# The buffer of each tile named by the plan's own times in a kernel with an S4D convolution and linear attention

## The chip, the core and the metric

The kernel runs on one core of a Trainium2 chip. TensorE (PE) multiplies matrices and writes into PSUM, a memory of eight banks; VectorE (DVE) and ScalarE (ACT) read PSUM and empty it; GpSimd (POOL) works on SBUF alone; SyncE (SP) issues the transfers (DMA). The engines run side by side, each through its own row of instructions, and wait for each other by semaphores. In the profile PEld is the loading of weights into TensorE, which overlaps the matmuls (PE).

The metric is the time of one execution on the device, in microseconds (us).

## What is computed

Two independent parts stand side by side in the output. A is a long convolution over 2048 positions with a kernel made from S4D parameters, by FFTs. B is linear attention with a learned feature map over 32 heads of 18 columns.

```python
def _A_ref(u, log_A_real, A_imag, C_real, C_imag, log_dt, D_skip):
    L = u.shape[1]
    dt = jnp.exp(log_dt)
    A = -jnp.exp(log_A_real) + 1j * A_imag
    C = (C_real + 1j * C_imag) * dt[:, None]
    P = jnp.exp((A * dt[:, None])[:, :, None] * pos[None, None, :])
    K = 2.0 * jnp.einsum("dn,dnl->dl", C, P).real
    y = irfft(rfft(u_t, 2 * L) * rfft(K, 2 * L)[None], 2 * L)[:, :, :L]
    return y.transpose(0, 2, 1) + u * D_skip[None, None, :]

def _B_ref(x, wqkv, w_phi, wo):
    q, k, v = ...
    pq = jnp.einsum("bhsd,hdf->bhsf", q, w_phi)
    pk = jnp.einsum("bhsd,hdf->bhsf", k, w_phi)
    phi_q = jnp.concatenate([_softmax(pq), _softmax(-pq)], axis=-1)
    phi_k = jnp.concatenate([_softmax(pk), _softmax(-pk)], axis=-1)
    kv = jnp.einsum("bhsf,bhsd->bhfd", phi_k, v)
    z = jnp.einsum("bhsf->bhf", phi_k)
    o = einsum(phi_q, kv) / (einsum(phi_q, z) + 1e-6)
    return o.reshape(B, S, D) @ wo

return jnp.concatenate([a, b], axis=-1)
```

Shapes: 2048 positions, 576 columns, 128 states; all float32.

## The kernel before

**Attention.** The 2048 rows are taken in 16 tiles of 128. A key tile multiplies x by the key and value weights, in three groups of 14 matmuls (`gemm`, line 537), each into one PSUM tile; DVE, ACT and POOL make the two softmaxes; 32 small matmuls (ps<-e,v, line 620) add to the sums over keys. Then 16 query tiles do the same for the queries, transpose, divide, and multiply by the output weights. Products are made more exact by splitting each factor into a rounded part and a rest (wh and wl for the weights).

**Convolution.** `u_first` (line 742) and `first` (line 730) are first FFT steps of the input and of the kernel; `group` (line 905) makes the kernel's values from waves (cs) and magnitudes, with three matmuls ps<-sel,mg (line 915) whose results ACT turns into exponentials (line 916) and DVE multiplies into cs and E (lines 922 to 927). `product` (line 981) takes eight blocks for each half of the columns: 16 matmuls ps<-ub,ff (line 1003), kernel-side matmuls ps<-kb,fk (line 1022), complex products into ac, and 16 matmuls back. `last` (line 1059) is the final step.

**The order.** All of this is recorded first, as a list of 2972 operations with an engine, an estimated length, the operations they depend on, and the tiles (`Buf`) they touch. The string `ORDER` says in which order they are laid out, and so the row of each engine; parts of A and B are interleaved in it. `Plan.run` walks through that order once. For each operation it works out an estimated start, the latest of its engine's time, its inputs' ends and the free times of the buffers that it takes, and then emits the instruction. Where it estimates that PE would stand idle, it emits filler matmuls into the tile about to be written (line 215).

**The buffers.** Every tile has a tag. A tag has a fixed number of buffers: `ps` has eight, the eight PSUM banks, through which all matmul results go; `small` seven, `cs` four, `e` and `x9` three, most others one or two. The plan keeps, for each tag, a list of the times at which its buffers come free (`free`). When a tile is first touched, the smallest of these times is taken off the list and delays the operation's estimated start; when the tile's last use has been emitted, the estimated end of its uses goes back on the list. These are numbers alone: the tile itself is asked of a pool with as many buffers as the tag has, and the pool chooses which one it gets. The framework then adds the waits: whoever first writes the tile waits for all readers of the tile that was in that buffer before.

Of the kernel before, what the change touches and what calls it, by code (L numbers as in the profile page):

```python
# [143 lines left out]
class Buf:  # L144


    def __init__(self, tag, shape, dt):
        self.tag, self.shape, self.dt = tag, shape, dt
        self.writers, self.readers, self.left, self.end, self.t = [], [], 0, 0.0, None
# [9 lines left out]
class Plan:  # L159
# [10 lines left out]
        self.ops, self.pools, self.free, self.unit, self.part = [], {}, {}, None, None  # L170

    def tag(self, name, pool, n):
        self.pools[name], self.free[name] = pool, [0.0] * n

    def at(self, name, k=0):
        self.unit, self.part = (name, k), None
# [4 lines left out]
    def buf(self, tag, shape, dt=F32):  # L181
        return Buf(tag, shape, dt)
# [35 lines left out]
    def run(self, order):  # L218


        ops = self.ops
        if sorted(int(x.rstrip("*")) for x in order) != list(range(len(ops))):
            raise RuntimeError("the order does not hold every operation once")
        at = {e: 0.0 for e in self.LAG}
        port = dict(dve=0.0, pool=0.0)
        self.warm, self.short, self.long = False, 0.0, 0.0

        def idle(t):
            self.short += max(0.0, t)
            if self.short > IDLE:  # L230
                self.warm, self.long = False, 0.0

        def busy(t, share):
            self.short = max(0.0, self.short + t * (1.0 - 2.0 * share))
            self.long += t * share
            if self.long > WARM and self.short <= IDLE:
                self.warm = True
        table, dma, end, mode = None, 0.0, [None] * len(ops), None
        for x in order:
            k, second = int(x.rstrip("*")), x.endswith("*")  # L240
            o = ops[k]
            e, cost = o[5] if second else o[:2]
            s = max([at[e], *(end[d] for d in o[3])])
            for b in o[4]:
                if b.t is None:
                    fr = self.free[b.tag]
                    b.t0 = min(fr)
                    fr.remove(b.t0)
                    s = max(s, b.t0)
                    b.t = self.pools[b.tag].tile(b.shape, b.dt, name=b.tag, tag=b.tag)  # L250
            if o[8] and e in port:
                s = max(s, port["pool" if e == "dve" else "dve"])
            if e == "act" and o[6] and table and o[6] != table:
                s += 1420.0
            table = o[6] or table
            fill = 0
            if e == "pe":
                t = at[e]
                if o[11] is not None:
                    t = max(t, 0.0 if o[12] else o[11].t0, self.zero_at)  # L260
                    idle(t - at[e])
                    c = FILL if self.warm else 2 * FILL
                    fill = max(0, min(100, int((s - 150.0 - t) // c)))
                    busy(fill * c, 1.0)
                    t += fill * c
                idle(s - t)
                cost = (cost + (20.0 if o[10] == mode else 95.0 + o[10][1] / 1.2)) * (1 if self.warm else 2)
                mode = o[10]
                busy(cost, o[7])
            self.emit(o, e, fill)  # L270
            at[e] = s + (560.0 if e == "sp" else cost)
            if o[8] and e in port:
                port[e] = at[e]
            if e == "sp":
                dma = max(dma, s + 1050.0) + cost
            end[k] = (max(dma, s + 1050.0 + 1.85 * cost) if e == "sp" else at[e]) + self.LAG[e]
            for b in o[4]:
                b.left -= 1
                b.end = max(b.end, end[k])
                if not b.left:  # L280
                    self.free[b.tag].append(b.end)
        self.end, self.time = end, max(end)


# [12 lines left out]
def c_dma(nbytes, run=4096):  # L297
    return nbytes / run * (0.35 + 0.0029 * run)
# [112 lines left out]
def body(tc, nc, i, out, ctx):  # L411
    pl = Plan()
    pe, dve, act, pool, sp = nc.tensor, nc.vector, nc.scalar, nc.gpsimd, nc.sync

    def tags(spec, space=None):
        kw = {} if space is None else dict(space=space)
        for n, names in spec.items():
            p = ctx.enter_context(tc.tile_pool(name=f"x{n}{len(pl.pools)}", bufs=n, **kw))
            for t in names.split():
                pl.tag(t, p, n)  # L420

    tags({1: "zero ident w1 w3 hp dsk kvb fT wh wl ks E sel dt th cre cim ax ay mx mn ld ldc",
          2: "v1 o ot pi mg ff ub kb zo us2 ac yo zi", 3: "e fk x9", 4: "cs", 7: "small"})
    tags({8: "ps"}, space=PSUM)
    tags({1: "gd kz", 5: "dram", 16: "xd"}, space=DRAM)
    B, op = pl.buf, pl.op

# [677 lines left out]
```

## Time and profile before

| | |
|---|---|
| three runs, median | 586.39 us |
| three runs, lowest and highest | 583.33 and 587.55 us |
| the profiled execution | 580.1 us |
| its span, from the first to the last instruction | 578.1 us |
| mean granted TensorE clock | 0.999 |

The lines that carry the prediction are shown in it. A line of the timeline gives start, length, engine, line of the kernel, operation, output<-inputs, shapes, a count of instructions merged, and in brackets how long the engine stood idle before it and what ended that. Nearly all matmuls have line 429, a helper, so they are told apart by their tiles: ps<-wh,x is a matmul of x with a weight. Copies out of PSUM have line 434.

### The profile page before, as it was taken

What the parts mean: (1) busy time and instruction counts of PE and PEld (TensorE: products, weight loads), DVE (VectorE), ACT (ScalarE), POOL (GpSimd) and SP (SyncE); (2) the same over time, 40 slices, a digit from 0 to 9 for tenths busy, and PEclk for the clock granted to TensorE, in tenths of its full rate; (3) what the DMA queues carried; (4) which work ended last, traced back from release to release, by engine and by line L of the source; (5) the groups of instructions that cost most, each with busy time, mean ns of one, the idle gap of its engine ahead of it and who ended that gap; (6) DMA issues with size and microseconds to landing.
All of it is one profiled execution on the core that took longest, in us unless ns stands there. A gap on an engine that the chain in (4) does not pass through costs nothing. (4 is left out here: it accounts for less than half of the span.)

```text
span 578.1 us, 18504 instructions
## 1 busy us (share of the span) xinstructions
PE 539.4 (93%) x7555; PEld 445.8 (77%) x7555; DVE 499.5 (86%) x1064; ACT 392.4 (68%) x674; POOL 288.6 (50%) x433
## 2 busy tenths in 40 slices
PE   3999899999889998989999999999999989889996
PEld 3998798899867788778777777667687966667984
DVE  4899899999889899999999999999978779778662
ACT  4779978687577999787778686999583433332331
POOL 0654586777667657860764656766302431122100
PEclk9999999999999999999999999999999999999999
DMA  8987751443356666437665765977477879898487
GB/s 228 301 302 255 226 205 69 129 135 97 111 133 206 202 206 195 151 96 203 210 223 167 232 240 156 252 218 226 132 253 236 225 247 302 261 298 263 164 277 214
DMA packets 91313, 119.21 MB, mean 206 GB/s; under 512 B 9826, under 2 KB 73186, under 8 KB 91230
## 3 DMA queue, kind: packets, MB, share of 16 engines
q1 hardware_dynamic: 91230, 118.04, 65.9%
q8 instruction: 59, 0.97, 0.7%
q14 instruction: 24, 0.20, 0.1%
HBM read 68.76 MB, written 49.26 MB: 204 GB/s over the span
## 5 line engine op out<-in xcount | busy, mean ns | idle before, releaser
L429 PE MATMUL ps<-wh,x 128*128 128x288 f32 (+2 forms) x1008 | 241.1, 319 | 5.3 <-ACT zi L434 1.8
L429 PEld LDWEIGHTS ps<-wh,x 128*128 128x128 f32 x1008 | 173.1, 188 | 16.6 <-DVE E L923 2.7
L429 PE MATMUL ps<-wl,x 128*128 128x288 f32 (+2 forms) x560 | 175.2, 313 | 0.0
L886 POOL TENSOR_TENSOR cs<-cs,pi 128x128 int32<-128x128 int32 (+4 forms) x180 | 116.4, 650 | 10.1
L429 PEld LDWEIGHTS ps<-wl,x 128*128 128x128 f32 x560 | 105.4, 188 | 1.5 <-issue 0.3
L916 ACT ACTIVATE ps<-ps 128x512 f32<-128x512 f32 x108 | 60.0, 588 | 12.9 <-PE ps L429 12.6
L577 POOL TENSOR_TENSOR o<-e 128x576 f32<-128x576 f32 x32 | 42.4, 1324 | 49.0 <-ACT e L574 42.6
L444 POOL TENSOR_TENSOR ac<-ac 128x288 f32<-128x288 f32 x40 | 32.8, 831 | 55.9 <-DVE ac L448 45.5
L448 DVE TENSOR_TENSOR ac<-us,ps 128x576 f32<-128x576 f32 x64 | 44.9, 746 | 7.2 <-PE ps L429 6.5
L922 DVE TENSOR_TENSOR cs<-ps,cs 128x1024 f32<-128x1024 f32 x36 | 43.8, 1216 | 7.0 <-ACT ps L916 7.0
L574 ACT ACTIVATE e<-e 128x1152 f32<-128x1152 f32 x32 | 37.3, 1168 | 10.2 <-DVE e L444 6.7
L923 DVE TENSOR_TENSOR E<-ps,cs 128x1024 f32<-128x1024 f32 x36 | 43.5, 1209 | 0.3 <-ACT ps L916 0.2
L429 PEld LDWEIGHTS ps<-E,cs 128*32 128x32 f32 x2304 | 34.2, 110 | 11.9 <-issue 3.5
L429 PEld LDWEIGHTS ps<-kvb,fT 126*128 126x128 f32 (+1 forms) x320 | 38.8, 189 | 5.3 <-issue 3.1
L429 PE MATMUL ps<-E,cs 128*32 128x64 f32 x2304 | 40.1, 220 | 2.9 <-DVE E L923 0.9
L429 PE MATMUL ps<-kvb,fT 126*128 126x133 f32 (+1 forms) x320 | 41.4, 278 | 0.2
L902 ACT ACTIVATE cs<-cs,hp 128x1040 f32<-128x1040 f32 x36 | 41.3, 1149 | 0.0
L429 PE MATMUL ps<-sel,mg 128*128 128x512 f32 x108 | 38.0, 430 | 3.6 <-DVE wl L496 1.6
L444 POOL TENSOR_TENSOR e<-small,e 128x576 f32<-128x576 f32 x20 | 23.3, 1167 | 33.7 <-DVE e L448 27.3
L429 PE MATMUL ps<-kb,fk 128*64 128x288 f32 x256 | 35.7, 414 | 4.2 <-DVE zo L434 1.6
L444 POOL TENSOR_TENSOR e<-e,small 128x576 f32<-128x576 f32 (+1 forms) x17 | 27.0, 1590 | 23.5 <-DVE small L448 17.1
L901 ACT ACTIVATE cs<-cs 128x1040 f32<-128x1040 int32 x36 | 38.3, 1064 | 0.2
(140 smaller groups left out, 1037.3 us busy)
## 6 DMA issues: line engine op xcount, KB each, us to landing
xd<-x SPq DMA_DIRECT2D x16, 576.0 KB, 4.7
dram<-zi SPq DMA_DIRECT2D x16, 576.0 KB, 3.1
dram<-zi SPq DMA_DIRECT2D x32, 288.0 KB, 4.5
x<-xd SPq DMA_DIRECT2D x16, 576.0 KB, 5.9
kb<-dram SPq DMA_DIRECT2D x32, 288.0 KB, 5.2
ub<-dram SPq DMA_DIRECT2D x32, 288.0 KB, 4.3
dram<-zo SPq DMA_DIRECT2D x32, 288.0 KB, 4.4
zi<-dram SPq DMA_DIRECT2D x16, 576.0 KB, 4.8
```

What stands on the lines that cost most here:

```text
L429: pe.matmul(o, l, r, start=start, stop=stop, skip_group_check=skip)
L444: op(eng, [c_dve(n[0]) if e == "dve" else c_pool(n[1]) for e in eng], lambda e: (dve if e == "dve" else pool).tensor_tensor(dst(), a(), b( ...
L448: op(eng, c_dve(n) if eng == "dve" else c_pool(n), lambda: e.tensor_tensor(dst(), a(), b(), op=alu), r=r, w=w, lock=eng == "pool" or not a ...
L574: op("act", c_act(1152) + 40, lambda: act.activation(e.t, e.t, AF.Exp), r=[e], w=[e], table="exp")
L577: op("pool", c_pool(470), lambda: pool.tensor_tensor(pair.t, e.t[:, :, :, 0:9], e.t[:, :, :, 9:18], op=ALU.add), r=[e], w=[pair], lock=True)
L886: op("pool", c_pool(2 * n * W), lambda n=n, j=j: pool.tensor_tensor(x()[:, :, :, n:2 * n], x()[:, :, :, 0:n], pi.t[:, j:j + 2, gs].bitcast ...
L901: act.activation(cs.t[:, 1], cs.t[:, 1].bitcast(I32), AF.Sin, scale=TURN)
L902: act.activation(cs.t[:, 0], cs.t[:, 0], AF.Sin, scale=-TURN, bias=hp.t)
L916: op("act", c_act(512), lambda: act.activation(ps.t, ps.t, AF.Exp), r=[ps], w=[ps], table="exp")
L922: op("dve", c_dve(64 * W), lambda: dve.tensor_tensor(F(), both(M.t), F(), op=ALU.mult), r=[M, cs], w=[cs])
L923: op("dve", c_dve(64 * W), lambda: dve.tensor_tensor(E.t[:, :, :, 32:64], both(up.t), cs.t[:, :, :, 0:32], op=ALU.mult), r=[up, cs], w=[E])
```

## The change

Each buffer gets a tag of its own. The plan's list of free times becomes a list of pairs of a time and the buffer's number; the smallest pair is taken, and the tile is asked of the pool under the tag with that number, of which there is one buffer only. So the buffer that a tile gets is the one whose estimated end was taken off the list. Pools are made with one buffer for each tag; the memory in all is the same.

```diff
     def tag(self, name, pool, n):
-        self.pools[name], self.free[name] = pool, [0.0] * n
+        self.pools[name], self.free[name] = pool, [(0.0, k) for k in range(n)]
...
                 if b.t is None:
                     fr = self.free[b.tag]
-                    b.t0 = min(fr)
-                    fr.remove(b.t0)
+                    slot = min(fr)
+                    fr.remove(slot)
+                    b.t0, b.slot = slot
                     s = max(s, b.t0)
-                    b.t = self.pools[b.tag].tile(b.shape, b.dt, name=b.tag, tag=b.tag)
+                    b.t = self.pools[b.tag].tile(b.shape, b.dt, name=b.tag, tag=f"{b.tag}{b.slot}")
...
                 if not b.left:
-                    self.free[b.tag].append(b.end)
+                    self.free[b.tag].append((b.end, b.slot))
...
-            p = ctx.enter_context(tc.tile_pool(name=f"x{n}{len(pl.pools)}", bufs=n, **kw))
+            p = ctx.enter_context(tc.tile_pool(name=f"x{n}{len(pl.pools)}", bufs=1, **kw))
```

The rows of the engines keep their instructions in the same order; lines behind the added one are numbered one higher. What differs is the buffers' addresses and the waits that follow from them. In the two built programs 224 of the 743 tiles of `ps` follow another tile in their bank than before, and so do 24 of 48 of zo, 16 of 32 of us2, 8 of 48 of ub, 8 of 34 of ac, 15 of 160 of small and 2 of 16 of yo; all other tags keep theirs. Three places of PE's row are shown with the semaphores that each instruction waits for (Activation_49 is ACT's, DVE_49 is DVE's, Pool_49 is POOL's, DMAHW a transfer's).

PE's row in a key tile, at the small matmuls ps<-e,v and the start of the next group (place A of the prediction); before:

```order
L429 MATMUL ps<-ks,w_173 64x288 [waits Activation_49] x2
L429 MATMUL ps<-ks,w_173 64x288 [waits DVE_49]
L429 MATMUL ps<-ks,w_173 64x288 [waits Activation_49]
L429 MATMUL ps<-ks,w_173 64x288 x4
L429 MATMUL ps<-e,v_2291 19x36 [waits Pool_49]
L429 MATMUL ps<-e,v_2291 19x36 x31
L429 MATMUL ps<-wh,x_2301 128x378 [waits Activation_49]
L429 MATMUL ps<-wl,x_2301 128x378
```

and now:

```order
L430 MATMUL ps<-ks,w_173 64x288 [waits Activation_49] x3
L430 MATMUL ps<-ks,w_173 64x288 [waits DVE_49]
L430 MATMUL ps<-ks,w_173 64x288 x4
L430 MATMUL ps<-e,v_2291 19x36 [waits Pool_49]
L430 MATMUL ps<-e,v_2291 19x36 x31
L430 MATMUL ps<-wh,x_2301 128x378 [waits DVE_49]
L430 MATMUL ps<-wl,x_2301 128x378
```

The group's first matmul waited for an ACT copy and now waits for a DVE copy; two of the ks matmuls have changed banks as well.

PE's row a little later, where two matmuls ps<-sel,mg follow the small ones (place B); before:

```order
L429 MATMUL ps<-sel,mg 128x512 [waits DVE_49,PE_49]
L429 MATMUL ps<-e,v_2806 19x36 [waits Pool_49]
L429 MATMUL ps<-e,v_2806 19x36 x31
L429 MATMUL ps<-sel,mg 128x512 [waits DVE_49]
L429 MATMUL ps<-sel,mg 128x512 [waits Activation_49]
L429 MATMUL ps<-wh,x_2400 128x396 [waits DVE_49]
```

and now:

```order
L430 MATMUL ps<-sel,mg 128x512 [waits DVE_49,PE_49]
L430 MATMUL ps<-e,v_2806 19x36 [waits Pool_49]
L430 MATMUL ps<-e,v_2806 19x36 x31
L430 MATMUL ps<-sel,mg 128x512 [waits Activation_49]
L430 MATMUL ps<-sel,mg 128x512 [waits DVE_49]
L430 MATMUL ps<-wh,x_2400 128x396 [waits DVE_49]
```

The two have swapped banks, and so the engines that they wait for.

PE's row in the third block of a product, the 16 matmuls ps<-ub,ff into four banks (place C); before:

```order
L429 MATMUL ps<-ub,ff 32x288 [waits DMAHW6_49,Activation_49]
L429 MATMUL ps<-ub,ff 32x288 [waits Activation_49]
L429 MATMUL ps<-ub,ff 32x288 [waits DMAHW4_49]
L429 MATMUL ps<-ub,ff 32x288 x5
L429 MATMUL ps<-ub,ff 32x288 [waits Activation_49]
L429 MATMUL ps<-ub,ff 32x288 [waits DVE_49]
L429 MATMUL ps<-ub,ff 32x288 x6
```

and now:

```order
L430 MATMUL ps<-ub,ff 32x288 [waits DMAHW6_49,Activation_49]
L430 MATMUL ps<-ub,ff 32x288
L430 MATMUL ps<-ub,ff 32x288 [waits DMAHW4_49]
L430 MATMUL ps<-ub,ff 32x288 x5
L430 MATMUL ps<-ub,ff 32x288 [waits Activation_49] x2
L430 MATMUL ps<-ub,ff 32x288 x6
```

The fourth bank, taken in the tenth matmul, was one that DVE read last, and is now one that ACT read last.

## The prediction

> **What bounds the kernel now.** I read the page first, then the chain of work that ended last, then who waits for whom on PE, and last the timeline around each place where PE stands still.
>
> ```profile
> span 578.1 us, 18504 instructions
> PE 539.4 (93%) x7555; PEld 445.8 (77%) x7555; DVE 499.5 (86%) x1064; ACT 392.4 (68%) x674; POOL 288.6 (50%) x433
> ```
>
> PE, the matmul engine, is busy for 93% of the span. Its idle time, 578.1 - 539.4 = 38.7 us, is the most that any change of waits can save.
>
> ```profile
> by line: PE ps L429 11.4%; PE ps L676 0.6%; PE ps L704 0.4%; issue 0.1%; DVE zo L434 0.1%; DVE yo L434 0.1%; PE ps L705 0.1%; DVE fT L434 0.0%; DVEq L434 0.0%
> ...
> 572.85 0.04 issue
> 572.89 0.46 DVE yo L434
> ```
>
> The chain, as far back as it was followed, is PE after PE up to the last copy: a matmul that starts earlier, and stays earlier, ends the kernel earlier. So what counts is which of PE's waits the change touches.
>
> ```profile
> PE ps L429 <- DMA fT<-in_wphi_dram: 7.2, 1, 7.2
> PE ps L429 <- ACT zi L434: 3.1, 4, 1.6
> PE ps L429 <- DVE E L923: 2.7, 6, 1.2
> ```
>
> The longest wait is for the first weights and has no bank in it. Behind it come matmuls that wait for a copy out of PSUM (zi, line 434) which has nothing to do with their inputs: they wait for the bank that the copy still reads. Those are the waits that another choice of banks can move.
>
> **The change, part by part.** It adds, removes and reorders no arithmetic instruction and no DMA; on each engine the operations stand as before. The plan's own times, and with them the filler matmuls of line 215, are the same too, since the smallest free time is still the one taken. What changes is which earlier tile a tile follows in its buffer: for 224 of the 743 PSUM tiles, and for some tiles of six SBUF tags (zo, ub, ac, us2, small, yo). For each PE stall I compare the end of the reader that PE waited for with the end of the reader of the bank that it now gets.
>
> Place A, a key tile after the small matmuls ps<-e,v:
>
> ```profile
> 172.93 0.35 DVE L434 COPY v<-ps 128x180 f32<-128x180 f32 x1 [1.00 <-PE ps L429]
> ...
> 174.07 0.39 ACT L434 ACTIVATE zi<-ps 128x288 f32<-128x288 f32 x1
> ...
> 174.51 0.19 PEld L429 LDWEIGHTS ps<-wh,x 128*128 128x128 f32 x1 [1.76 <-ACT zi L434]
> 174.51 0.44 PE L429 MATMUL ps<-wh,x 128*128 128x378 f32 x1 [1.63 <-ACT zi L434]
> ```
>
> Before, the matmul waits for the zi copy, which ends at 174.46. Now its bank is the one that the v copy read, free at 173.28. Gross gain 174.46 - 173.28 = 1.18 us. What is late next is here:
>
> ```profile
> 183.38 0.35 DVE L434 COPY ks<-ps 128x256 f32<-128x256 f32 x1
> 183.39 1.24 POOL L886 TENSOR_TENSOR cs<-cs,pi 128x128 int32<-128x128 int32 x2
> 183.78 0.58 ACT L916 ACTIVATE ps<-ps 128x512 f32<-128x512 f32 x1 [0.51 <-PE ps L429]
> 183.82 0.19 PEld L429 LDWEIGHTS ps<-wh,x 128*128 128x128 f32 x1
> ```
>
> The weight load at 183.82 waits, before and after, for the ks copy that ends at 183.73. It has 0.09 us to spare, so PE gives the 1.18 us back there: net 0 for A by itself. But the ACT exponentials of the matmuls just ahead of it start early, and ACT is full from there on:
>
> ```profile
> 183.30:194.20 10.90, 10.82 (x178) 8.52 (x177) 10.21 (x24) 10.37 (x15) 9.37 (x14) 1.00 0.70 216
> ```
>
> The columns are length, PE, PEld, DVE, ACT and POOL busy: ACT works 10.37 of 10.90 us, so a start that is 1.2 us earlier comes out about 1.2 us earlier at 194. That carries place B:
>
> ```profile
> 192.51 0.82 DVE L434 COPY zi<-ps 128x288 f32<-128x288 f32 x2
> ...
> 194.18 0.39 ACT L434 ACTIVATE zi<-ps 128x288 f32<-128x288 f32 x1
> ...
> 193.62 0.19 PEld L429 LDWEIGHTS ps<-sel,mg 128*128 128x128 f32 x1
> 194.62 0.19 PEld L429 LDWEIGHTS ps<-sel,mg 128*128 128x128 f32 x1 [0.81 <-ACT zi L434]
> ```
>
> Two sel matmuls swap banks: the first now takes the one that the ACT copy reads until 194.57, the second the one that DVE had left at about 193. With ACT unchanged the wait only moves one matmul forward. With ACT 1.2 us early the copy ends near 193.4, before the first needs it, and the 0.81 us go. I take 0.81, because ACT's stretch is nearer to full than to slack; the other end is 0.
>
> Place C, the first products of a block (line 1005):
>
> ```profile
> 326.11 0.41 ACT L434 ACTIVATE ot<-ps 128x288 f32<-128x288 f32 x1 [1.35 <-PE ps L429]
> ...
> 328.01 0.45 DVE L448 TENSOR_TENSOR e<-ps,small 128x288 f32<-128x288 f32 x1
> ...
> 327.04 1.15 PE L429 MATMUL ps<-ub,ff 64*32 64x288 f32 x18
> 328.52 0.71 PE L429 MATMUL ps<-ub,ff 64*32 64x288 f32 x14 [0.32 <-DVE e L448]
> ...
> 328.51 0.18 PEld L429 LDWEIGHTS ps<-ub,ff 64*32 64x32 f32 x14 [0.86 <-DVE e L448]
> ...
> 398.59 1.20 PE L429 MATMUL ps<-ub,ff 64*32 64x288 f32 x32
> ```
>
> The step took 329.23 - 327.04 = 2.19 us; the same 32 matmuls take 1.20 us where nothing holds them. The bank now follows the ot copy, done at 326.52. Gain 0.99 us.
>
> Place D, the kernel side of a product (line 1023), two waits in one step:
>
> ```profile
> 403.83 1.01 ACT L434 ACTIVATE zo<-ps 128x288 f32<-128x288 f32 x3
> ...
> 405.06 0.71 PE L429 MATMUL ps<-kb,fk 128*64 128x288 f32 x4 [0.31 <-PE ps L676]
> 406.14 1.68 PE L429 MATMUL ps<-kb,fk 128*64 128x288 f32 x12 [0.38 <-DVE E L923]
> ...
> 504.11 2.16 PE L429 MATMUL ps<-kb,fk 128*64 128x288 f32 x16
> ```
>
> It took 407.82 - 405.06 = 2.76 us against 2.16 us undisturbed. The banks now follow zo copies, done by 404.84. Gain 0.60 us.
>
> The smaller places:
>
> ```profile
> 107.63 0.19 PEld L429 LDWEIGHTS ps<-sel,mg 128*128 128x128 f32 x1 [0.39 <-DVE e L448]
> ...
> 163.09 0.19 PEld L429 LDWEIGHTS ps<-wh,x 128*128 128x128 f32 x1 [0.70 <-DVE zi L434]
> ...
> 164.89 1.21 DVE L923 TENSOR_TENSOR E<-ps,cs 128x1024 f32<-128x1024 f32 x1
> ...
> 166.32 0.19 PEld L429 LDWEIGHTS ps<-wh,x 128*128 128x128 f32 x1 [0.44 <-DVE E L923]
> ...
> 274.84 0.19 PEld L429 LDWEIGHTS ps<-sel,mg 128*128 128x128 f32 x1 [0.63 <-DVE e L448]
> ...
> 277.65 1.22 DVE L923 TENSOR_TENSOR E<-ps,cs 128x1024 f32<-128x1024 f32 x1
> ...
> 279.02 0.37 PE L429 MATMUL ps<-wh,x 128*128 128x288 f32 x1 [0.18 <-DVE E L923]
> ...
> 418.00 0.19 PEld L429 LDWEIGHTS ps<-sel,mg 128*128 128x128 f32 x1 [0.27 <-DVE o L448]
> ```
>
> Their gross is 0.39 + 0.70 + 0.63 + 0.27 = 1.99 us at most. Most of it is given back at the next DVE result. The lead from 163.09 ends at 166.32, where DVE's E lands at 166.10: 0.2 us survive. The lead from 274.84 ends at 279.02, where E lands at 278.87: 0.1 us. At 107.63 the group right behind inherits the bank that is still read: 0.1 us. Behind 418.00 I find no such place: 0.27 us. Together about 0.7 us.
>
> The SBUF side I cost at nothing:
>
> ```profile
> SPq L993 <- PE ps L429: 26.9, 19, 4.0
> ```
>
> SP waits 26.9 us to refill ub, but both ub tiles of a product are released by the same matmul step, so swapping the two moves no load, and nothing in SP's queue stands behind a longer wait. For ac, us2, small and yo no wait of PE names the earlier owner of the buffer.
>
> Sum: A 0, B 0.81, C 0.99, D 0.60, smaller 0.7: 3.1 us. Against the profiled execution's own 580.1 us (span 578.1 and 2.0 around it) that is 577.0. The runs shown have their median at 586.39, 6.3 above that execution, so on their scale I forecast 583.3 us, 0.5% less. Ends of the sum: everything gross kept is 1.18 + 0.81 + 0.99 + 0.60 + 1.99 = 5.6 us; nothing kept is 0; below nothing, see the slower rival.
>
> One rule bears on the size. I took step lengths and weight-load (PEld) gaps and not the idle of the matmul rows, which at B, C and D is less: C shows 0.32 us there where the step lost 0.99. The Trainium skill ("Perfetto Trace Analysis", Identifying the Most-Contended Engine) says that matmul busy time is a poor measure, since matmuls are pipelined, and that weight-load busy time is better. By matmul idle C and D alone would give 0.32 + 0.38 = 0.7 us in place of 1.59, and the sum would be about 2.2; the row of the undisturbed step agrees with the skill here.
>
> **The rivals.**
> Faster by more than 1%: PE keeps every lead, because DVE, which is fed by PE, moves forward as ACT does. The gain is the gross 5.6 us, 580.8 on the scale of the runs. Against it speaks that DVE is busy 86% of the span and that its copies at 166.10, 183.73 and 278.87 come just before PE needs them.
> No change: every lead is given back as at 183.82, and the two steps C and D find other DVE results late. The gain is under 1 us: 586 us.
> Slower than before: the plan's times say which bank is free first, and on the chip another reader ends last. Place B shows the price: if ACT does not come early there, the first sel matmul waits from 193.62 to 194.57 where it did not wait, 0.95 us, and the second's 0.81 are not saved. It decides when such late readers number three or more among the 224 tiles: C, D and the smaller places give 2.3 us, and 3 x 0.95 is 2.9. With five of them the time is 586.39 - 2.3 + 4.8 = 588.9 us. Against it: in this trace B is the only place where a bank's new reader ends more than 0.2 us after the tile's first write.
>
> **How the numbers follow.** Forecast (net gain 1 to 5.5 us) 0.69, everything kept or more 0.13, no change 0.12, slower 0.06. A measurement of this kernel can tell about 1%, 5.9 us, from no change. Faster by over 1% takes all of the gross and a little from the runs' own scatter: 0.14. Slower by over 1%, over 592 us, would take nine late readers: 0.04 with scatter. The rest, 0.82, is within 1%. The range takes the sum's ends, 580.8 to 586.4, and the scatter of the runs shown, 583.33 to 587.55 about 586.39, as far as needed: 578.5 to 587.5.
>
> **What would show it.** Right: no idle of 0.8 us or more ahead of the wh,x load of place A, the step at C back to 1.20 us, the one at D to about 2.2, the wait ahead of the second sel of place B gone, and a new or longer wait for the ks copy where the 183.82 load stands. Wrong: the idle ahead of the first sel of B grown to about 0.95; C or D still long, with another releaser; or SP's wait for line 993 longer. If PE's total idle falls by much less than 3 us while A, C and D are cured, the give-backs were under-counted; if it falls by more than 5, DVE moved forward with PE.

## The result and the profile after

| kernel | median, runs | ratio to before |
|---|---|---|
| before | 584.11 us, 11 (581.31 to 587.55) | |
| changed | 578.50 us, 11 (573.87 to 581.22) | 0.9898, 95% interval 0.9865 to 0.9930 |

The change saves 1.0%, between 4.1 and 7.9 us; the forecast was 3.1 us net. The forecast time of 583.3 us stood on the 586.39 us of the three runs known then; eleven runs put the kernel before at 584.11 us, so the gains are compared here and not the times. Some executions are over 1.5% slower than the fastest of their kernel; the ratios in this document leave these out and so differ a little from the quotients of the medians. The profiled execution of the changed kernel took 576.53 us, at a mean granted clock of 0.996.

The page of the changed kernel, its span and the busy times:

```profile
span 574.5 us, 18495 instructions
PE 540.1 (94%) x7555; PEld 446.6 (78%) x7555; DVE 499.3 (87%) x1064; ACT 392.6 (68%) x674; POOL 289.4 (50%) x433
```

The work is the same, and PE's idle time is 574.5 - 540.1 = 34.4 us, where it was 38.7. Its waits (total, count, longest), the lines that stood first before:

```profile
PE ps L430 <- DMA fT<-in_wphi_dram: 7.7, 1, 7.7
PE ps L430 <- DVE E L924: 2.3, 5, 1.3
...
PE ps L430 <- ACT zi L435: 1.5, 3, 0.8
```

Every line number is one higher than before. The wait for the zi copies has halved, from 3.1 to 1.5 us. The timeline at place A, then at place B:

```profile
172.68 0.35 DVE L435 COPY v<-ps 128x180 f32<-128x180 f32 x1 [0.99 <-PE ps L430]
...
173.08 0.19 PEld L430 LDWEIGHTS ps<-wh,x 128*128 128x128 f32 x1 [0.57 <-DVE v L435]
...
192.83 0.39 ACT L435 ACTIVATE zi<-ps 128x288 f32<-128x288 f32 x1
...
193.27 0.30 PEld L430 LDWEIGHTS ps<-sel,mg 128*128 128x128 f32 x2 [0.71 <-ACT zi L435]
```

At A, PE now waits for the v copy, 0.57 us in place of 1.76. At B a wait for ACT's zi copy is still there, 0.71 us; it has moved from the second sel matmul to the first. Places C and D, the steps that the forecast said would return to 1.20 and about 2.2 us (the transposes ahead of D with it):

```profile
324.52 1.20 PE L430 MATMUL ps<-ub,ff 64*32 64x288 f32 x32
...
399.68 1.09 PE L677 MATMUL ps<-ident,e 128*126 128x128 f32 x8
400.70 2.16 PE L430 MATMUL ps<-kb,fk 128*64 128x288 f32 x16
```

Both did.

### The profile page after: what moved, and what is told of

Same layout as the page of the kernel before. It is cut to its first block, busy times and chain, and to the rows that moved or that the text cites. A ratio compares the mean times of both kernels' runs of the same rounds, so it can differ in the third digit from the quotient of the medians.

```text
span 574.5 us, 18495 instructions
## 1 busy us (share of the span) xinstructions
PE 540.1 (94%) x7555; PEld 446.6 (78%) x7555; DVE 499.3 (87%) x1064; ACT 392.6 (68%) x674; POOL 289.4 (50%) x433
## 4 chain that ended last, share of the span: by engine, by line
PE 56%; DVE 25%; ACT 10%; DMA 4%; issue 4%; SPq 1%; DVEq 0%; ACTq 0%
PE ps L430 52%; DVE cs L923 3%; DVE e L445 2%; PE ps L677 2%; DVE E L924 2%; ACT ps L917 2%; DMA kb<-dram 1%; DVE small L567 1%; ACT cs L897 1%; DVE e L449 1%; DMA fT<-in_wphi_dram 1%; DVE x L445 1%; DVE small L568 1%; DVE small L579 1%; ACT cs L903 1%
```

## The experiments

Two ways of reading are used. The first is the ratio of times. Single runs of one kernel scatter by some 2 us, and part of that goes with the clock. A line was fitted to 159 runs (76 of before, 23 of the change, 12 each of e3 to e6 and e8), with a level for each kernel and one common slope: 0.01 less of mean granted clock goes with 1.75 us more. By that fit the change brings -5.2 +- 0.9 us (95%).

The second is finer, and looks at single places. The row of every engine is the same in all kernels, so the nth matmul of one is the nth of another. I took, over a short stretch around a place, how much longer or shorter it took from one weight load to another than the median of three traces: before, e1, and e4 (in which 27 tiles have other banks than in before, none of them at A to D, 275 or 345).

**First: which memory, and how far do runs repeat.** e1 and e2 are the two kernels again. e3 names buffers of PSUM alone, e4 of SBUF alone.

```diff
-b.t = self.pools[b.tag].tile(b.shape, b.dt, name=b.tag, tag=f"{b.tag}{b.slot}")
+b.t = self.pools[b.tag].tile(b.shape, b.dt, name=b.tag, tag=f"{b.tag}{b.slot}" if b.tag == "ps" else b.tag)
-p = ctx.enter_context(tc.tile_pool(name=f"x{n}{len(pl.pools)}", bufs=1, **kw))
+p = ctx.enter_context(tc.tile_pool(name=f"x{n}{len(pl.pools)}", bufs=1 if space is PSUM else n, **kw))
```

This is e3 against the changed kernel; e4 has the two conditions the other way round.

> The kernel before once more, for the scatter and a second trace. Theory 1 (the gain is PE's waits for PSUM banks, cured at places A to D and the smaller ones; what is beyond the forecast 3.1 us is the clock and chance of the single executions): ratio to before 1.000 +- 0.003, and the second trace shows PE idle at the same places, ahead of the ps<-wh,x of place A (about 1.7 us in weight loads), the second ps<-sel,mg of place B (0.8), in the step of place C (2.2 against 1.2 us) and of place D (2.8 against 2.2). Theory 2 (the stalls at A to D are chance of one execution): they are elsewhere in this trace.

> The changed kernel once more. Theory 1: ratio 0.990 +- 0.003; places A to D cured again; the lead over before grows to 4 to 6 us by the start of the last stage (about 499 us), and where the granted clock stays near 1.0 there, it is kept to the end. Rival (the last stage, whose loads come from DRAM, eats the lead whatever the clock): the lead falls by 2 to 3 us behind 499 us with the clock at 1.0 too.

> Only the PSUM tag names its buffers; the SBUF tags are left to the pool. Theory 1 (all of the gain is PSUM banks): ratio 0.990, within 0.002 of the changed kernel. Rival (the SBUF tags, ub and zo above all, bring what the forecast lacked, 2.5 us): ratio about 0.9945.

> Only the SBUF tags name their buffers; the PSUM banks are left to the pool, which then gives 27 of the 743 PSUM tiles another bank than before. Theory 1: ratio 1.000 +- 0.002. Rival (SBUF tags bring the 2.5 us that the forecast lacked): ratio about 0.9955.

| run | median | ratio to before (583.85) |
|---|---|---|
| e1, before again | 583.29 | 0.9994 (0.9962 to 1.0025) |
| e2, the change again | 577.91 | 0.9916 (0.9887 to 0.9946) |
| e3, PSUM alone | 577.24 | 0.9896 (0.9861 to 0.9932) |
| e4, SBUF alone | 583.95 | 1.0004 (0.9976 to 1.0032) |

These are 12 runs each. The PSUM banks bring the gain; naming the SBUF buffers has no effect that these runs could show (-1.4 to +1.9 us).

e1's trace shows the waits of before again: 1.76 us ahead of A's load, 0.82 us ahead of the second sel load of B, 2.20 us for the step at C and 2.76 us for the one at D. They belong to the kernel and not to one execution. In e2's trace A, C and D gain again (C only 0.70 us), but its lead over before is 2.3 us at 499 us and not the 4 to 6 us expected; the last section says where it went.

**Second: which places.** The next four kernels name the bank of each of the 743 PSUM tiles by a table. With the pool's own banks in it, it would give the kernel before; exchanging the banks of two tiles, and with them all that follow in these banks, changes what these two wait for and nothing else. Line numbers are 15 higher than before.

```diff
+BANKS = ("0765432147062517603247516237150622507164152041257471520674561475...")
-b.t = self.pools[b.tag].tile(b.shape, b.dt, name=b.tag, tag=b.tag)
+tag = b.tag
+if tag == "ps":
+    tag, banks = f"ps{banks[0]}", banks[1:]
+b.t = self.pools[b.tag].tile(b.shape, b.dt, name=b.tag, tag=tag)
```

> The pool's banks for all PSUM tiles, named one by one, with only five tiles (and the five that take over their old banks) moved as in the change: the key tile of place A, the first sel tile of place B, the step of place C, the two tiles of place D. Theory 'the places add up, and those the forecast named carry half': the aligned traces of the first batch put A and B together at -0.81, C at -0.99, D at -0.98, so -2.8 us, ratio about 0.995. Rival 'the forecast's places carry nearly all and the rest is scatter': -5 us or more, ratio 0.991 or less. Rival 'leads are lost unless the whole order of banks is changed': within 1 us of before. In the trace: C's step 1.20 us in place of 2.19, D's 2.16 in place of 2.76.

> The reverse: the banks of the change for all PSUM tiles but those of the four named places, which keep the banks that the pool gave. Theory 'half lies elsewhere': places near 107, 163, 200, 275, 287, 302, 345 and 418 us sum to about -2.5 us, ratio about 0.996. Forecast as on record: only the smaller places, -0.7 us, ratio 0.999. In the trace the step near 345 us (ub,ff) runs in about 1.0 to 1.2 us in place of 1.66, and C and D are as slow as before (2.19, 2.76).

> The pool's banks with three places moved: A alone (without B), the sel tile at 274.84, and the ub,ff step at 345. Forecast as on record: A's 1.18 us are given back whole at the load of 183.82 (the ks copy), and the lead of 274.84 falls to 0.1 at 279.02; nothing at 345. Theory from the aligned traces: of A's 1.18 about 0.47 are given back by 184 and 0.7 stay to 193, where the second sel matmul still waits for ACT's zi copy, which itself comes about as much earlier; 0.53 stay from 274.84; 0.71 come at 345. Against the run of before, PE's lead is then about 0.7 us at 193 us, grows by 0.5 at 275 and by 0.7 at 345. One look, total not decisive.

> Each PSUM tile takes, of the banks free at its place in the order, the one whose last reader ended first in the trace of the changed kernel, in place of by the plan's own times: 115 tiles follow another tile than in the change. In that trace only two tiles among them start within 0.25 us of their bank's release and would gain over 0.5 us (the tiles at 174.9 and 192.5 us). Theory 'the plan's times already pick well': the same as the change, ratio to before 0.988 to 0.992, at most 1 us better than the change. Rival 'the plan's times leave much': 2 us or more better than the change, ratio below 0.987.

| run | median | ratio to before (582.96) | by the fit, us |
|---|---|---|---|
| e5, A, B, C, D alone | 580.80 | 0.9977 (0.9946 to 1.0008) | -2.4 +- 1.2 |
| e6, all but A, B, C, D | 581.36 | 0.9962 (0.9929 to 0.9995) | -2.9 +- 1.2 |
| e7, A, 275 and 345 alone | 579.91, one run | | |
| e8, banks by the trace | 578.44 | 0.9913 (0.9879 to 0.9946) | -5.2 +- 1.2 |

e5, e6 and e8 have 12 runs each. About half of the gain lies at the four places that the forecast worked out, half at others. By its ratio alone e5 can't be told from before; the fit, and the places below, can. The same by place, in us:

| place (stretch, on the clock of before) | forecast, net | changed | e2 | e3 | e5 | e6 | e7 |
|---|---|---|---|---|---|---|---|
| near 163 (161 to 170) | -0.2 | -0.37 | -0.19 | +0.20 | +0.34 | -0.18 | -0.02 |
| A and B (170 to 203) | -0.81 | -1.12 | -1.12 | -0.99 | -1.16 | -0.34 | -1.17 |
| near 275 (272 to 284) | -0.1 | -0.58 | -0.60 | -0.59 | +0.01 | -0.59 | -0.43 |
| near 302 (298 to 305) | 0 | -0.13 | -0.14 | -0.13 | 0.00 | -0.14 | +0.01 |
| C (325 to 331) | -0.99 | -0.98 | -0.70 | -1.00 | -0.42 | 0.00 | -0.01 |
| near 345 (343 to 348) | 0 | -0.72 | -0.73 | -0.72 | -0.01 | -0.72 | -0.57 |
| D (403 to 410) | -0.60 | -0.98 | -0.98 | -0.98 | -0.94 | -0.05 | +0.03 |
| near 418 (415 to 420) | -0.27 | -0.35 | -0.36 | -0.35 | 0.00 | -0.35 | +0.01 |

The column of the changed kernel sums to -5.2 us; the forecast for the same rows to -3.0. e6 gains 0.34 at A too, though A and B have the pool's banks in it: A's load comes 0.40 earlier there; which other tile brings this wasn't followed. At 107 us, where the forecast had 0.1, the stretch took 0.2 us less in e1 too, whose banks are the pool's; that is not the change.

e8 took the place of the plan's estimated ends with measured ones, and is not better than the change. The plan's times already pick as well as that, and no version came out ahead of the change by more than the scatter.

**Third: what a bank costs that comes free late.** The table again, with the bank that came free second, and last, by the trace of the changed kernel.

> Each PSUM tile takes the bank that came free second by the trace of the changed kernel (of those free at its place in the order; the only one where there is one). By that trace 108 tiles would then start before their bank's last reader has ended, 79 of them by over 0.2 us, 55.7 us in all if every wait stood by itself. Theory 'waits for banks add up, since DVE and ACT move with PE': most of it, 40 us or more slower than the change. Theory 'a wait ahead of PE lets the readers catch up, so later waits shrink': 15 to 35 us slower than the change. Rival 'an order of banks that is off by one costs little': under 6 us slower than the change, about as fast as before.

> The same with the bank that came free last of all: 284 tiles would start early by the trace of the changed kernel, 250 us in all if every wait stood by itself. Theory 'waits add up': over 150 us slower. Theory 'the readers catch up': 60 to 150 us slower. Rival 'PE, DVE and ACT have slack enough': under 30 us slower.

```profile
span 588.1 us, 18491 instructions
...
PE 546.2 (93%) x7555; PEld 446.1 (76%) x7555; DVE 497.9 (85%) x1064; ACT 395.0 (67%) x674; POOL 288.4 (49%) x433
```

```profile
span 708.7 us, 18501 instructions
...
PE 579.9 (82%) x7555; PEld 464.5 (66%) x7555; DVE 499.0 (70%) x1064; ACT 397.1 (56%) x674; POOL 287.3 (41%) x433
```

e9 (first fence) has a median of 591.64 us in four runs, 1.0144 of before (1.0074 to 1.0214); e10 (second) 707.22 us in two runs, 1.2105 (1.1984 to 1.2226). Against the 578.4 us of e8, which used the same list of times, that is 13 us for e9 and 129 us for e10, of 55.7 and 250 us of waits that each would cost alone. Both expectations that waits add up fell. e9 lies between the rival's 6 us and the 15 us at which the middle one begins, nearer to the middle one; e10 lies within its middle one. Much of what single late banks would cost is absorbed: followed in steps of 1 us, PE loses 29 us against the changed kernel in some stretches of e9's trace and gets 15 back in others (e2, the changed kernel itself, loses 7 and gets 5 back). How much of e10's 129 us is waiting alone isn't known: its granted clock was 0.952, and PE's rows were busy for 579.9 us in place of 540.1.

## Why the forecast was too small

The direction and the mechanism of the gain were right: it is PE's waits for banks, the SBUF buffers have no part in it that could be seen, and the waits at A, C and D went as was said. The sum fell short by about 2 us, in four terms: A with B (0.3), 275 (0.5), 345 (0.7) and D (0.4). Behind the first two is one wrong step: the forecast let a lead of PE end at the next result of DVE, as if DVE's results came at fixed times. The other two were waits that it didn't see as waits for a bank.

**The lead at A is not given back.** The forecast put A at 0, because the load at 183.82 would wait for a ks copy that stays where it was, and gave B 0.81 because ACT alone comes early. Measured: A's load comes 1.18 us earlier, as forecast, but only 0.39 of it are lost by 184 us, since the ks copy on DVE had moved forward too:

```profile
182.50 0.36 DVE L435 COPY ks<-ps 128x256 f32<-128x256 f32 x1
...
182.91 0.19 PEld L430 LDWEIGHTS ps<-wh,x 128*128 128x128 f32 x1 [0.22 <-DVE ks L435]
```

The copy came 0.88 us earlier than the 183.38 of before, 0.63 of it beyond the lead that PE had ahead of A. The load does wait for it now, as was forecast, but 0.22 us. ACT did come early. In e7, which moves A and leaves B as the pool had it, the timeline at B reads:

```profile
194.37 0.39 ACT L449 ACTIVATE zi<-ps 128x288 f32<-128x288 f32 x1
...
194.80 0.19 PEld L444 LDWEIGHTS ps<-sel,mg 128*128 128x128 f32 x1 [0.45 <-ACT zi L449]
```

PE of this execution ran 1.34 us behind the one of before at 166 us, so zi at 194.37 stands for 193.03 on the clock of before, where it was 194.18: 1.15 us early. The second sel matmul still waits for it, and PE's total lead after it, at 203 us, is 1.17 us. With A and B exchanged (e5) it is 1.16 there. So A is worth all of the 1.1 to 1.2 us, and B nothing: PE was itself 0.8 us early at the first sel, and the copy, which bounds one sel or the other, was not early enough to be out of the way. That the forecast's 0.81 for the two together lies near the 1.12 measured is luck: it gave A nothing and B everything.

**Nor at 275.** The forecast ended this lead at 279.02, where E on DVE would land no earlier than before. After:

```profile
272.96 0.53 PEld L430 LDWEIGHTS ps<-sel,mg 128*128 128x128 f32 x3
...
275.72 1.23 DVE L924 TENSOR_TENSOR E<-ps,cs 128x1024 f32<-128x1024 f32 x1
...
277.06 0.19 PEld L430 LDWEIGHTS ps<-wh,x 128*128 128x128 f32 x1 [0.54 <-ACT e L575]
```

The sel load went from 274.84 to 272.96, 1.88 us earlier with the leads from before it, and E from 277.65 to 275.72, 1.93 earlier: DVE moved with PE. The wait at 279.02 did not swallow the lead, and 0.58 us are kept where the forecast had 0.1. This is the mechanism of the first rival (every lead kept), against which the forecast took DVE's 86% as a sign that DVE holds back. At these two places DVE held PE back by 0.4 us of 1.18 and not at all: its ks copy came earlier by part of PE's lead, its E by all of it.

**A place that was not seen: 345.** Before:

```profile
344.11 1.21 DVE L923 TENSOR_TENSOR E<-ps,cs 128x1024 f32<-128x1024 f32 x1
...
344.74 1.66 PE L429 MATMUL ps<-ub,ff 64*32 64x288 f32 x23
...
345.43 0.68 PEld L429 LDWEIGHTS ps<-ub,ff 64*32 64x32 f32 x28 [0.56 <-issue]
```

e6, which has the bank of the change here:

```profile
340.13 1.21 DVE L938 TENSOR_TENSOR E<-ps,cs 128x1024 f32<-128x1024 f32 x1
...
340.76 0.67 PEld L444 LDWEIGHTS ps<-ub,ff 64*32 64x32 f32 x32 [0.17 <-issue]
340.77 1.20 PE L444 MATMUL ps<-ub,ff 64*32 64x288 f32 x32
```

Before, one tile of the step lies in the bank that DVE's E reads until 344.11 + 1.21 = 345.32, and the weights of its matmul load at 345.43. The row says "issue", that is, a wait for nothing that the profile shows, because this matmul waits for two readers at once and one of the waits is an instruction of its own ahead of it. The forecast had looked only at waits that name a reader. With the other bank the step takes its 1.20 us, and 0.72 us are gained, although E ends 0.58 us after the step's start in both (345.32 - 344.74 and 341.34 - 340.76). All waits of weight loads under that name (total, count, longest), before and then in the changed kernel:

```profile
PEld ps L429 <- issue: 28.7, 79, 2.0
```

```profile
PEld ps L430 <- issue: 26.3, 77, 1.8
```

It fell by 2.4 us, of which only the 0.56 us here were followed to a bank. The sum of these rows stood in the list of waits that the forecast read, and was not broken down.

**D was counted from its first matmul.** The forecast compared step lengths, 2.76 and 2.16 us, and left out what lies ahead of the step. Before:

```profile
403.65 1.09 PE L676 MATMUL ps<-ident,e 128*126 128x128 f32 x8
...
404.28 0.68 DVE L925 TENSOR_TENSOR E<-ps,cs 128x512 f32<-128x512 f32 x1
...
405.03 0.23 PEld L429 LDWEIGHTS ps<-kb,fk 128*64 128x64 f32 x4 [0.52 <-PE ps L676]
```

The step's first bank was read by this E until 404.96, and the load starts at 405.03, though the profile puts the wait down to PE's own transposes. In the changed kernel the same E ends at 400.95, after the step has begun at 400.70. From the start of the transposes to that of the step it is 405.06 - 403.65 = 1.41 us before and 400.70 - 399.68 = 1.02 us after: 0.39 us more, which with the 0.60 make the 0.98 measured. One more row that the forecast did not have, 302 with 0.13 us, wasn't followed.

**What was right in size:** C (0.99 forecast, 0.98 and 1.00 in two of three traces), 418 (0.27 and 0.35), the smaller net at 163 within its scatter. By the idle time of their matmul rows C and D would have been worth 0.7 us together, and they gave 1.96. So the 38.7 us of idle rows are not the most that waits can cost, as the forecast took them: at C the rows show 0.32 us idle, and 0.99 was lost. The Trainium skill ("Perfetto Trace Analysis", Identifying the Most-Contended Engine) says that TensorE's matmul busy time is not a good measure of how close a kernel is to its limit, because pipelined instructions look smaller in the trace. C and D agree with it.

**The slower rival** did not come about, though its mechanism exists: e9 and e10 are slower by it. To add up 0.95 us for each late reader was too much, as e9 shows: about 13 us for 79 tiles that would wait over 0.2 us, whose waits alone come to most of 55.7 us.

**The signs** named ahead were mixed. A, C and D showed the right ones, and so did the new wait for the ks copy. The wait at B did not go: 0.71 us stand ahead of the first sel, nearer to the sign of being wrong (0.95). PE's idle time fell by 4.3 us, under the 5 that was to tell that DVE moved with PE, and yet it did at 275.

The places' 5.2 us and the 5.6 us between the two medians agree within the interval; the 0.4 us between them are not told apart from scatter.

## What to carry to other kernels

Where matmul results go through few PSUM banks, look up, for each matmul that starts late, which instruction read its bank last, also where the profile names no reader ("issue") or names PE itself: here two such rows held 1.1 of 5.2 us. Before you write a lead off at the next wait, ask whether the instruction that ends this wait was itself waiting for the engine that is now early; if it was, it comes early too. Which free bank a tile takes is worth about 1% here between the pool's choice and the plan's, nothing that these runs can show between the plan's and a measured order, and 2% more time than the plan's for the one that is second to come free.

## What was not expected of the hardware

**The granted clock dips in single executions.** The stretch from 500 to 520 us of before, of e1 (the same kernel) and of the changed kernel (columns: length, PE, PEld, DVE, ACT and POOL busy, granted clock, share of the DMA engines, GB/s):

```profile
500.00:520.00 20.00, 18.38 (x276) 12.75 (x261) 14.72 (x31) 6.83 (x17) 4.66 (x6) 1.00 0.85 273
```

```profile
500.00:520.00 20.00, 17.15 (x196) 12.15 (x196) 13.17 (x29) 5.14 (x13) 4.53 (x5) 0.91 0.81 240
```

```profile
500.00:520.00 20.00, 18.14 (x218) 12.38 (x217) 12.46 (x26) 6.03 (x15) 3.53 (x5) 0.91 0.89 270
```

The same program has 1.00 here in one execution and 0.91 in another. The changed kernel's own lead over the trace of before falls in part through such a dip, from 6.1 us at 499 us to 3.6 at the end, so the difference of two profiled executions (580.1 and 576.53) understates this change.

Other traces dip elsewhere. e2, e3, e5 and e8 each lose about 2 us between 203 and 230 us, where their granted clock is 0.94 and that of before and of the changed kernel 1.00; e4 loses 1.44 us between 170 and 203, at 0.95. This is where most of e2's lead went. Behind 499 us, at a clock of 1.00, e2 loses only 0.6 us more, so the last stage by itself does not eat a lead of 2 to 3 us. In the traces of before, of the change and of e1 to e9 there are ten such dips (the start and the end of the span left out), and each begins 0.1 to 2.2 us after PE's matmul row has stood idle for more than 1.1 us. Most idle stretches of that length are followed by none; why one is and the next is not isn't settled.

**Behind a bank a transfer can wait.** Place C in e5:

```profile
325.26 1.77 PE L444 MATMUL ps<-ub,ff 64*32 64x288 f32 x32
...
325.84 0.66 PEld L444 LDWEIGHTS ps<-ub,ff 64*32 64x32 f32 x28 [0.44 <-DMA ub<-dram]
```

The bank is free, and the step takes 1.77 us and not 1.20, because its ub lands late by 0.44 us. In the changed kernel and in e3 C gains its 0.98 and 1.00 us, in e2 only 0.70. The forecast costed the ub transfers at nothing; at this place they are next in line behind the bank, and in e5's execution took more than half of what it gave.
